# A state-space layer beside a gated MLP: the discretisation factors move from B to C, and B and C are transposed by DMA without fences

## The chip, the core and the metric

One core of a Trainium2 chip runs the whole program. The time is the device time of one execution in microseconds, the median of three runs. The core's engines work side by side: TensorE (PE) multiplies matrices, VectorE (DVE) and ScalarE (ACT) do elementwise work, GpSimd (POOL) does a little here, and SyncE (SP) issues all DMAs. Each engine carries out its own list of instructions in order and waits on semaphores for the others.

## The reference, cut to what matters

```python
xn = layernorm(x)                                  # x: 1 x 2048 x 512
dt = exp(log_dt); Lam_bar = exp(dt * Lam)          # 512 complex states
B_bar = ((Lam_bar - 1) / Lam)[:, None] * (B_re + 1j*B_im)
Bu = xn @ B_bar.T                                  # 2048 x 512, complex
h[t] = Lam_bar * h[t-1] + Bu[t]
y = 2 * real(h @ (C_re + 1j*C_im).T) + xn * Dskip
out = x + y + (gelu(xn @ w_gate) * (xn @ w_up)) @ w_down   # w: 512 x 1376, 1376 x 512
```

The factor `(Lam_bar - 1) / Lam` is one complex number for each state. It may stand on the rows of B, ahead of the recurrence, or on the columns of C, behind it: the recurrence is linear and its own factor is diagonal, so the result is the same.

## The kernel before, in words

The 2048 rows are cut into four blocks of 512. For each block b the kernel has these steps:

- **LN(b)** (lines 560 to 589): statistics (`bn_stats`, L563) and subtraction (L575) on DVE, the power on POOL (L569), the scaling `ln_mul` partly on DVE (L583) and partly on ACT (L587).
- **TR(b)** (lines 591 to 622): the transposed XNT[b]. Block 0 goes through PE; blocks 1 to 3 go through four DMA transposes each (L596).
- **GU(b)** (L676): for each of 11 tiles `ft` of the 1376 columns, four matmuls of 128x512 for the gate and four for up (L686), then on ACT the gelu (L690) and the eviction `evU` (L694), and on DVE their product `hmul` (L696). The gelu of tile ft writes one of three buffers, so it waits for the hmul of tile ft - 3.
- **BU(b)** (L624): B_bar times XNT[b], eight groups of four matmuls (L633), each evicted from PSUM by ACT (`evBu`, L637).
- **CHAIN(b)** (L640): the recurrence on DVE. The complex values are turned by tables of cosine and sine (`pre_c` L646, `pre_s` L647, `pre_re`, `pre_im`), scanned in eight real scans (L657), and turned back (`post_c` L669 to `post_im` L673).
- **DN(b)** (L704): for each of four row tiles, 11 matmuls with w_down, 4 small ones for Dskip and 8 with the transposed C (L730). DVE adds x (L742), and SP stores.

PSUM has eight banks, used in turn by all groups of matmuls: a group waits until the eviction of the eighth group before it is done.

**B.** Before, the factor is put on B while it is transposed. B_re and B_im are loaded as they are (L435). DVE makes 12 diagonal 128x128 matrices `diag` out of the factor (L514). PE multiplies slices of B by them, 64 matmuls of 128x128 called `prepB` (L533), which transposes and scales in one step, and ACT evicts the eight results (`evB`, L538). These pieces are put between the tiles of GU(0) from ft 4 on.

**C.** C_re and C_im are transposed by DMA from HBM (L450), unscaled, after everything that the first part loads.

**Tables.** `tables_fn` (L545) makes the sine and cosine tables: DVE steps, then `sint` on ACT (L551), then `f2` on DVE (L554), which overwrites what sint read, then `cost` on ACT (L556). pre_c needs both tables and the evictions of BU(0).

**Fences.** `S.dma(..., fenced=True)` makes a DMA wait for all earlier DMAs, and all later ones wait for it (lines 122 to 131). All DMA transposes are fenced.

**The order.** A planner (`schedule`, L136) holds PE's and SP's instructions in the order in which the program lists them, and chooses ACT's and DVE's order by estimated costs and due times. An edit thus changes the order on ACT and DVE beyond its own lines. Memory of the first part (raw B, diagonals, tables' steps) is reused later for the states `SS` and for CHAIN's temporaries, so the first evictions of BU(0) wait until the raw data there has been read.

PE's order is: warm-up, TR(0), GU(0) with prepB, BU(0), BU(1), GU(1), BU(2), DN(0), GU(2), DN(1), BU(3), GU(3), DN(2), DN(3).

Of the kernel before, what the change touches and what calls it, by code (L numbers as in the profile page):

```python
# [313 lines left out]
def build(nc, ins, out, dbg=None, stage=99, opts=None):  # L314
    dbg = dbg or {}
    opts = opts or {}
    with ExitStack() as es:
        E = es.enter_context
        S = Sched(nc, es)
        S.fence_slack = float(opts.get("fence_slack", FENCE_SLACK))  # L320
# [60 lines left out]
        BN = A.alloc("BN", [2, KP, D], BF16)  # L381
        DG = A.alloc("DG", [KP, 3, 128], BF16)
# [19 lines left out]
        if "DN" in dbg:  # L402
            DNB = A.alloc("DNB", [4, D], F32)
# [7 lines left out]

        do_ssm = stage >= 3
# [13 lines left out]
        if do_ssm:  # L426
            for T_, nm in ((LDT, "A_log_dt"), (LRE, "A_Lambda_re"), (LIM, "A_Lambda_im")):
                S.dma(ld_param(T_, ins[nm]), 1024, writes=[T_], tag="ld_" + nm)
# [4 lines left out]
        if do_ssm:  # L433
            for c, nm in enumerate(("A_B_re", "A_B_im")):
                S.dma(lambda e, c=c, nm=nm: e.dma_start(BN.ap[:, c], ins[nm].rearrange("(s p) d -> p s d", p=128)),  # L435
                      512 * 1024, writes=[A.sub(BN, "BN%d" % c, c)], tag="ld_" + nm)
# [8 lines left out]
        XT_DMA = opts.get("xt_dma", (1, 2, 3))  # L445

        def load_CT():
            CTc = [A.sub(CT_all, "CTc%d" % c, c) for c in range(2)]
            for c, nm in enumerate(("A_C_re", "A_C_im")):
                S.dma(lambda e, c=c, nm=nm: e.dma_start_transpose(CTc[c].ap, ins[nm]),  # L450
                      opts.get("ct_bytes", 2.0) * 512 * 1024, writes=[CTc[c]], tag="tr_" + nm, fenced=True)
# [10 lines left out]
        if do_ssm:  # L462
            POOL(lambda e: e.iota(IOTJ.ap, [[1, 512]], base=0, channel_multiplier=0), 600, [], [IOTJ], "iotj")
# [13 lines left out]
        last_table_op = None  # L477
        GATE = {"before_gelu": []}
        if do_ssm:
            (A_, TH, RRr, LBR, LBI, N1, TAa, TBb, DEN, RDEN, TC, TD, NRE, TE, TF, NIM, CR, CI) = range(18)  # L480
            pa = lambda i: PA[i].ap
            t1 = ACT(lambda e: e.activation(DTB.ap, LDT.ap, ACTF.Exp), d_act(4), [LDT], [DTB], "exp_dt")
            V(lambda e: e.tensor_tensor(pa(A_), DTB.ap, LRE.ap, ALU.mult), D_TINY, [DTB, LRE], [PA[A_]])
            V(lambda e: e.tensor_tensor(pa(TH), DTB.ap, LIM.ap, ALU.mult), D_TINY, [DTB, LIM], [PA[TH]])
            t2 = ACT(lambda e: e.activation(pa(RRr), pa(A_), ACTF.Exp), d_act(4), [PA[A_]], [PA[RRr]], "exp_a", after=[t1])
            w16 = lambda a, b_: W16.ap[:, a:b_]
            W16p = [A.sub(A.alloc("W16v", [4, 4], F32, at=W16.lo), "W16_%d" % i, i) for i in range(4)]
            V(lambda e: e.tensor_scalar(w16(0, 4), pa(TH), 1.0 / TWO_PI, None, ALU.mult), D_TINY, [PA[TH]], [W16p[0]])
            V(lambda e: e.tensor_scalar(w16(4, 8), pa(TH), 512.0 / TWO_PI, None, ALU.mult), D_TINY, [PA[TH]], [W16p[1]])
            V(lambda e: e.tensor_scalar(w16(8, 16), w16(0, 8), 0.25, None, ALU.add), D_TINY, W16p[0:2], W16p[2:4])  # L490
            V(lambda e: e.tensor_copy(KI.ap, W16.ap), D_TINY, W16p, [KI])
            V(lambda e: e.tensor_tensor(FRC.ap, W16.ap, KI.ap, ALU.subtract), D_TINY, W16p + [KI], [FRC])
            t3 = ACT(lambda e: e.activation(SC16.ap, FRC.ap, ACTF.Sin, scale=SIN_SCALE), d_act(16), [FRC], [SC16], "sin16", after=[t2])
            GATE = {"before_gelu": [t3]}
            sinT, sinP, cosT, cosP = (SC16.ap[:, 4 * i:4 * i + 4] for i in range(4))
            V(lambda e: e.tensor_tensor(pa(LBR), pa(RRr), cosT, ALU.mult), D_TINY, [PA[RRr], SC16], [PA[LBR]])
            V(lambda e: e.tensor_tensor(pa(LBI), pa(RRr), sinT, ALU.mult), D_TINY, [PA[RRr], SC16], [PA[LBI]])
            V(lambda e: e.tensor_scalar(pa(N1), pa(LBR), -1.0, None, ALU.add), D_TINY, [PA[LBR]], [PA[N1]])
            V(lambda e: e.tensor_tensor(pa(TAa), LRE.ap, LRE.ap, ALU.mult), D_TINY, [LRE], [PA[TAa]])
            V(lambda e: e.tensor_tensor(pa(TBb), LIM.ap, LIM.ap, ALU.mult), D_TINY, [LIM], [PA[TBb]])  # L500
            V(lambda e: e.tensor_tensor(pa(DEN), pa(TAa), pa(TBb), ALU.add), D_TINY, [PA[TAa], PA[TBb]], [PA[DEN]])
            V(lambda e: e.reciprocal(pa(RDEN), pa(DEN)), 150, [PA[DEN]], [PA[RDEN]])
            V(lambda e: e.tensor_tensor(pa(TC), pa(N1), LRE.ap, ALU.mult), D_TINY, [PA[N1], LRE], [PA[TC]])
            V(lambda e: e.tensor_tensor(pa(TD), pa(LBI), LIM.ap, ALU.mult), D_TINY, [PA[LBI], LIM], [PA[TD]])
            V(lambda e: e.tensor_tensor(pa(NRE), pa(TC), pa(TD), ALU.add), D_TINY, [PA[TC], PA[TD]], [PA[NRE]])
            V(lambda e: e.tensor_tensor(pa(TE), pa(LBI), LRE.ap, ALU.mult), D_TINY, [PA[LBI], LRE], [PA[TE]])
            V(lambda e: e.tensor_tensor(pa(TF), pa(N1), LIM.ap, ALU.mult), D_TINY, [PA[N1], LIM], [PA[TF]])
            V(lambda e: e.tensor_tensor(pa(NIM), pa(TE), pa(TF), ALU.subtract), D_TINY, [PA[TE], PA[TF]], [PA[NIM]])
            V(lambda e: e.tensor_tensor(pa(CR), pa(NRE), pa(RDEN), ALU.mult), D_TINY, [PA[NRE], PA[RDEN]], [PA[CR]])
            V(lambda e: e.tensor_tensor(pa(CI), pa(NIM), pa(RDEN), ALU.mult), D_TINY, [PA[NIM], PA[RDEN]], [PA[CI]])  # L510
            DGs = [[A.sub(A.sub(DG, "DGs%d" % s, s), "DG%d_%d" % (s, q), q) for q in range(3)] for s in range(KP)]
            for s in range(KP):
                for q, (src_i, fac) in enumerate(((CR, 2.0), (CI, 2.0), (CI, -2.0))):
                    V(lambda e, s=s, q=q, src_i=src_i, fac=fac: e.tensor_scalar(  # L514
                        DGs[s][q].ap, IDN.ap, PA[src_i].ap[:, s:s + 1], fac, ALU.mult, ALU.mult),
                      d_dve_ts4x(128), [IDN, PA[src_i]], [DGs[s][q]], "diag")

            BNc = [A.sub(BN, "BN%d" % c, c) for c in range(2)]

            PREP_ITEMS = []  # L520

            def prep_fn():
              for c in range(2):
                  for dk in range(KD):
                    def item(c=c, dk=dk):
                      bank = next_bank()
                      pairs = ((0, 0), (1, 2)) if c == 0 else ((1, 0), (0, 1))

# [224 lines left out]
        if do_ssm:  # L753
            PREP_holder()
# [34 lines left out]
        if do_ssm:  # L789
            BU(2); CHAIN(2)  # L790
# [79 lines left out]
```

## Time and profile before

| what | value |
|---|---|
| median of three runs | 191.8 us (191.75 to 192.15) |
| span of the profiled execution | 190.1 us |
| PE busy | 183.3 us (96%) |
| DVE busy | 152.9 us (80%) |
| ACT busy | 88.6 us (47%) |
| prepB: 64 matmuls on PE (L533) | 4.2 us busy |
| evB: 8 evictions on ACT (L538) | 4.3 us busy |
| diag: 12 on DVE (L514) | 2.0 us busy |
| DMA of C_re, C_im: issue to landing | 4.0 and 4.1 us |

The profile comes from one execution. Its times count from the start of its span, and its span is shorter than the measured time by what lies around it: 191.8 - 190.1 = 1.7 us, taking the median. The PE row counts each matmul from its start to its modelled end, so neighbouring ones overlap; in the chain of work that ended last, the same 64 prepB matmuls have four pieces of 0.89 us.

### The profile page before, as it was taken

Reading aid. Unit: us, or ns where it says so; the run is one execution under the profiler, and the core shown is the slowest. Engines: PE = TensorE matmul, PEld = TensorE weight load, DVE = VectorE, ACT = ScalarE, POOL = GpSimd, SP = SyncE. Lnnn points to the kernel's source line nnn. Section 1 sums busy time; section 2 is a strip of 40 time slices with the busy share of each in tenths; the row PEclk is TensorE's granted clock in tenths of the full one; section 3 lists DMA queues with packets and bytes.
Section 4 is the critical chain, followed back from the end, with each engine's and each line's share of the span. In section 5 each row is a group of like instructions: output and inputs, shape, how many; then the busy total and the mean of one; then the engine's idle time right before and its main releaser. Section 6 shows DMA issues by size and latency. Waiting matters only on the chain.

```text
span 190.1 us, 2549 instructions
## 1 busy us (share of the span) xinstructions
PE 183.3 (96%) x944; PEld 87.6 (46%) x944; DVE 152.9 (80%) x265; ACT 88.6 (47%) x149; POOL 5.0 (3%) x10
## 2 busy tenths in 40 slices
PE   3989999999999999999999999999999999999993
PEld 1434664444444444444444444444444444444451
DVE  5869887089999999999999989999999999411111
ACT  2297988899996473000567910017676304000000
POOL 1200200002000000000002000000000000000000
PEclk9999999999999999999999999999999999999999
DMA  4899212784422000000000221000000000100100
GB/s 111 212 349 347 49 28 55 245 276 112 110 55 55 3 0 0 28 28 31 28 2 0 54 48 41 28 33 22 0 3 0 0 0 0 55 31 32 51 28 29
DMA packets 22908, 12.26 MB, mean 64 GB/s; under 512 B 13328, under 2 KB 22896, under 8 KB 22896
## 3 DMA queue, kind: packets, MB, share of 16 engines
q1 hardware_dynamic: 22896, 12.10, 22.7%
q8 instruction: 7, 0.11, 0.2%
q14 instruction: 5, 0.04, 0.1%
HBM read 7.38 MB, written 2.10 MB: 50 GB/s over the span
## 4 chain that ended last, share of the span: by engine, by line
PE 96%; DMA 1%; DVE 1%; issue 0%; DVEq 0%
PE PS L686 40%; PE PS L730 36%; PE PS L633 15%; PE PS L769 3%; PE PS L533 2%; DMA arena<-in_A_x_dram 1%; PE PS L609 0%; DVE arena L616 0%; DVE arena L742 0%; DVEq L281 0%
## 5 line engine op out<-in xcount | busy, mean ns | idle before, releaser
L686 PE MATMUL PS<-arena 128*128 128x512 bf16 (+1 forms) x352 | 77.3, 379 | 0.9 <-DVE arena L616 0.9
L730 PE MATMUL PS<-arena 128*128 128x512 bf16 (+2 forms) x368 | 69.8, 351 | 0.0
L686 PEld LDWEIGHTS PS<-arena 128*128 128x128 bf16 (+1 forms) x352 | 35.0, 100 | 40.7 <-issue 1.0
L730 PEld LDWEIGHTS PS<-arena 128*128 128x128 bf16 (+1 forms) x368 | 33.3, 98 | 35.9
L690 ACT ACTIVATE arena<-PS 128x512 bf16<-128x512 f32 (+1 forms) x44 | 26.4, 599 | 35.1 <-PE PS L686 23.3
L657 DVE TENSOR_TENSOR_SCAN arena<-arena 128x512 bf16<-128x512 f32 x32 | 38.5, 1253 | 0.0
L694 ACT ACTIVATE arena<-PS 128x512 bf16<-128x512 f32 (+1 forms) x44 | 26.3, 597 | 6.7 <-PE PS L686 6.4
L742 DVE TENSOR_TENSOR arena<-PS,arena 128x512 bf16<-128x512 f32 x16 | 10.9, 685 | 21.4 <-PE PS L730 21.3
L633 PE MATMUL PS<-arena 128*128 128x512 bf16 x128 | 28.1, 379 | 0.0
L637 ACT ACTIVATE arena<-PS 128x512 bf16<-128x512 f32 x32 | 17.5, 618 | 22.4 <-PE PS L633 22.1
L696 DVE TENSOR_TENSOR arena<-arena 128x512 bf16<-128x512 bf16 (+1 forms) x44 | 17.6, 418 | 3.6 <-ACT arena L694 3.6
L633 PEld LDWEIGHTS PS<-arena 128*128 128x128 bf16 x128 | 12.5, 98 | 15.0
L563 DVE BATCH_NORM_STATS2 arena<-arena 128x6 f32<-128x512 bf16 x16 | 9.9, 679 | 1.2 <-DMA arena<-in_A_x_dram 1.2
L669 DVE TENSOR_TENSOR arena<-arena 128x4096 bf16<-128x4096 bf16 x4 | 9.1, 2286 | 0.0
L646 DVE TENSOR_TENSOR arena<-arena 128x4096 bf16<-128x4096 bf16 x4 | 9.1, 2285 | 0.0
L670 DVE TENSOR_TENSOR arena<-arena 128x4096 bf16<-128x4096 bf16 x4 | 9.1, 2286 | 0.0
L647 DVE TENSOR_TENSOR arena<-arena 128x4096 bf16<-128x4096 bf16 x4 | 9.1, 2284 | 0.0
L769 PE MATMUL PS<-arena 128*128 128x512 bf16 x16 | 5.8, 543 | 2.9 <-DMA arena<-in_A_x_dram 2.9
L587 ACT ACTIVATE arena<-arena 128x512 bf16<-128x512 bf16 x10 | 7.1, 721 | 1.6 <-DVE arena L570 1.6
L569 POOL TENSOR_TENSOR arena<-arena 128x4 bf16<-128x4 bf16 x4 | 4.0, 1010 | 98.6 <-DVE arena L565 98.6
L554 DVE SCALAR_TENSOR_TENSOR arena<-arena 128x2048 f32<-128x2048 f32 x1 | 2.3, 2292 | 4.5 <-ACT arena L551 4.5
L575 DVE TENSOR_SCALAR arena<-arena 128x512 bf16<-128x512 bf16 x16 | 5.0, 347 | 0.1
(70 smaller groups left out, 72.7 us busy)
## 6 DMA issues: line engine op xcount, KB each, us to landing
out_dram<-arena SPq DMA_DIRECT2D x16, 128.0 KB, 1.7
arena<-in_A_x_dram SPq DMA_DIRECT2D x3, 512.0 KB, 5.5
arena<-in_B_w_down_dram SPq DMA_DIRECT2D x1, 1280.0 KB, 7.5
arena<-in_B_w_gate_dram SPq DMA_DIRECT2D x2, 512.0 KB, 5.5
arena<-in_B_w_up_dram SPq DMA_DIRECT2D x2, 512.0 KB, 6.5
arena<-in_A_x_dram SPq DMA_DIRECT2D x4, 128.0 KB, 2.2
arena<-in_A_B_re_dram SPq DMA_DIRECT2D x1, 512.0 KB, 7.4
arena<-in_A_B_im_dram SPq DMA_DIRECT2D x1, 512.0 KB, 7.9
```

The lines of the kernel that those rows point to most:

```text
L563: V(lambda e, tt=tt: e.bn_stats(ST[tt].ap, X[tt].ap), d_dve_1x(512), [X[tt]], [ST[tt]], "bnst")
L633: ins_ = e.matmul(PS[bank][:, :], BBT[c][dk].ap[:, 128 * s:128 * (s + 1)], XNT[b].ap[:, dk, :], start=(dk == 0), stop=(dk == KD - 1))
L637: ACT(lambda e, bank=bank, k3=k3, s=s, c=c: e.activation(SSc[k3][s][c].ap, PS[bank][:, :], ACTF.Copy), d_act(512), [BANK[bank]], [SSc[k3][ ...
L646: V(lambda e: e.tensor_tensor(TA.ap, ssb.ap, cos4, ALU.mult), d_dve_tt2x(4096), [ssb, COST], [TA], "pre_c")
L657: V(lambda e, g=g, rb=rb, init=init: e.tensor_tensor_scan(g.ap, rb, g.ap, init, ALU.mult, ALU.add), d_dve_scan(512), [g, PA[RRr]] + ([CARc ...
L686: ins_ = e.matmul(PS[bank][0:m, :], W.ap[:, dk, 128 * ft:128 * ft + m], XNT[b].ap[:, dk, :], start=(dk == 0), stop=(dk == KD - 1))
L690: GATE["last_gelu"] = ACT(lambda e, bg=bg, kk=kk, m=m: e.activation(GG[kk].ap[0:m, :], PS[bg][0:m, :], ACTF.Gelu_apprx_tanh), d_act(512), ...
L694: ACT(lambda e, bu=bu, kk=kk, m=m: e.activation(UPB[kk].ap[0:m, :], PS[bu][0:m, :], ACTF.Copy), d_act(512), [BANK[bu]], [UPB[kk]], "evU")
L696: V(lambda e, kk=kk, m=m, ft=ft, k2=k2: e.tensor_tensor(HTt[k2][ft].ap[0:m, :], GG[kk].ap[0:m, :], UPB[kk].ap[0:m, :], ALU.mult), d_dve_tt ...
L730: ins_ = e.matmul(o_, l_, r_, start=(n == 0), stop=(n == len(mms) - 1))
L742: V(lambda e, bank=bank, ko=ko, tt=tt: e.tensor_tensor(OUTB[ko].ap, PS[bank][:, :], X[tt].ap, ALU.add), d_dve_1x(512), [BANK[bank], X[tt]] ...
L769: ins_ = e.matmul(PS[wb][:, :], IDN.ap, X[0].ap, start=True, stop=True)
```

## The change

- The factor is put on C, not on B. `CR` and `CI` are made twice as large as before at once, and a third value `NCI = -CI` is added. The 12 diag, the 64 prepB and the eight evB are gone.
- B_re, B_im, C_re and C_im are all transposed by DMA from HBM, in `load_BC`, listed after ft 2 of GU(0) and ahead of TR(1): on SP they come right behind the loads of w_gate and w_up. The plain loads of B are gone.
- `scale_C`, listed after GU(0), makes the scaled C: for each of four slices and for the real and imaginary part one step `c_im` on ACT (128x512, bf16 to f32, with a factor for each partition) and one step `c_re` on DVE (multiply by a factor and add, 128x512). The f32 results lie in four buffers in turn.
- No DMA is fenced any more. The transposes of one TR(b) still wait for one another, because each declares the whole of XNT[b] as written.
- Options and debug code are taken out; this moves no instruction.

In the changed program, ACT's order around the change is: evU of ft 9, four c_im, gelu of ft 10, four c_im, evU of ft 10, nine evBu, sint, five evBu, cost, two evBu, GU(1). In GU(1) the gelu of ft 9 stands after four evictions of BU(2), and that of ft 10 after two more. DVE's order is: LN(1) ahead of most of the small steps for the factor, the table steps, eight c_re, LN(2), f2, three of the four statistics of LN(3), pre_c.

```diff
-        BN = A.alloc("BN", [2, KP, D], BF16)
-        DG = A.alloc("DG", [KP, 3, 128], BF16)
+        CRAW_all = A.alloc("CRAW", [2, KP, D], BF16)
+        CTMP_all = A.alloc("CTMP", [4, D], F32)
...
-                S.dma(lambda e, c=c, nm=nm: e.dma_start(BN.ap[:, c], ins[nm].rearrange("(s p) d -> p s d", p=128)),
-                      512 * 1024, writes=[A.sub(BN, "BN%d" % c, c)], tag="ld_" + nm)
...
-        def load_CT():
...
-                S.dma(lambda e, c=c, nm=nm: e.dma_start_transpose(CTc[c].ap, ins[nm]),
-                      opts.get("ct_bytes", 2.0) * 512 * 1024, writes=[CTc[c]], tag="tr_" + nm, fenced=True)
+        def load_BC():
+            for dst, nms in ((BBT_all, ("A_B_re", "A_B_im")), (CRAW_all, ("A_C_re", "A_C_im"))):
+                for c, nm in enumerate(nms):
+                    b_ = CRAW[c] if dst is CRAW_all else A.sub(BBT_all, "BBTc%d" % c, c)
+                    S.dma(lambda e, b_=b_, nm=nm: e.dma_start_transpose(b_.ap, ins[nm]),
+                          2 * 512 * 1024, writes=[b_], tag="tr_" + nm)
...
+        def scale_C():
+            for s in range(KP):
+                for c, (f_im, f_re) in enumerate(((NCI, CR), (CR, CI))):
+                    t = CTMP[(2 * s + c) % 4]
+                    ACT(lambda e, s=s, t=t, f_im=f_im: e.activation(
+                        t.ap, CRAW[1].ap[:, s, :], ACTF.Copy, scale=PA[f_im].ap[:, s:s + 1]),
+                        d_act(512, 1), [CRAW[1], PA[f_im]], [t], "c_im")
+                    V(lambda e, s=s, c=c, t=t, f_re=f_re: e.scalar_tensor_tensor(
+                        CT[c][s].ap, CRAW[0].ap[:, s, :], PA[f_re].ap[:, s:s + 1], t.ap, ALU.mult, ALU.add),
+                      d_dve_1x(512), [CRAW[0], PA[f_re], t], [CT[c][s]], "c_re")
...
-                        opts.get("xt_bytes", 1.2) * 128 * 1024, reads=[XN[tt % 8]], writes=[xd], tag="tr_x%d" % b, fenced=True)
+                        1.2 * 128 * 1024, reads=[XN[tt % 8]], writes=[xd], tag="tr_x%d" % b)
...
         for ft in range(KF):
             GU(0, [ft])
-            if ft >= opts.get("prep_from", 4):
-                prep_some(2)
-            if ft == opts.get("tr1_at", 2):
+            if ft == 2:
+                load_BC()
                 TR(1)
                 late_loads()
-        prep_some(99)
-        if do_ssm:
-            load_CT()
+        scale_C()
```

## Prediction

> **What bounds the kernel now.** I read the page, then TensorE's (PE's) waits, the chain that ended last, and the timeline of VectorE (DVE) and ScalarE (ACT) from 33 to 73 us. All times are us from the start of the profiled span.
>
> ```profile
> span 190.1 us, 2549 instructions
> PE 183.3 (96%) x944; PEld 87.6 (46%) x944; DVE 152.9 (80%) x265; ACT 88.6 (47%) x149; POOL 5.0 (3%) x10
> ```
>
> PE's waits have two rows, both before 10.5 us:
>
> ```profile
> PE PS L769 <- DMA arena<-in_A_x_dram: 2.9, 1, 2.9
> PE PS L686 <- DVE arena L616: 0.9, 1, 0.9
> ```
>
> So PE sets the end and never stands still after 10.47. The chain (start, length) gives its timetable:
>
> ```profile
> 10.47 8.79 PE PS L686 x40
> 19.27 0.89 PE PS L533 x16
> ...
> 33.20 13.81 PE PS L633 x64
> 47.02 18.99 PE PS L686 x88
> 66.01 6.91 PE PS L633 x32
> 72.92 17.31 PE PS L730 x92
> ```
>
> BU(0) and BU(1) start at 33.20, GU(1) at 47.02, BU(2) at 66.01, DN(0) at 72.92. What matters is how near the others are. From the timeline:
>
> ```profile
> 35.58 1.28 ACT L551 ACT_TABLE_LOAD   x1
> 36.87 1.91 ACT L551 ACTIVATE arena<-arena 128x2048 bf16<-128x2048 f32 x1
> ...
> 38.82 2.29 DVE L554 SCALAR_TENSOR_TENSOR arena<-arena 128x2048 f32<-128x2048 f32 x1 [4.47 <-ACT arena L551]
> ...
> 46.04 2.28 DVE L646 TENSOR_TENSOR arena<-arena 128x4096 bf16<-128x4096 bf16 x1
> ...
> 70.32 1.22 DVE L673 TENSOR_TENSOR arena<-arena 128x2048 bf16<-128x2048 bf16 x1
> ```
>
> sint (ACT) releases f2 (DVE), then CHAIN(0) begins with pre_c at 46.04 and ends with post_im at 71.54, 25.5 us without a gap. DN(0) reads its result and starts at 72.92: **the slack is 1.4 us**, although the page shows no wait there. Later slacks are wide: CHAIN(1) ends at 99.8 for DN(1) at 109.2, CHAIN(2) at 134.4 for DN(2) at 152.4, CHAIN(3) at 160.7 for DN(3) at 169.8, and XNT3 lands at about 115 for BU(3) at 126.5.
>
> **Part 1, PE.** The 64 prepB matmuls go: four pieces of 0.89 in the chain, 3.56 us, all on the path. A group of four matmuls takes 18.99/22 = 0.863. If nothing else were late, PE would reach BU(0) at 29.64, BU(1) at 36.55, GU(1) at 43.46, BU(2) at 62.45, DN(0) at 69.36, and the time would be 191.8 - 3.6 = 188.2. That is the lower limit.
>
> **Part 2, DMA.** The two plain B loads (1 MB) go. Four 512x512 transposes come, issued right behind the last weight load instead of at 43.7 behind fences. The C transposes of before show their price, 4.0 and 4.1 to landing, 1.9 of issue on SP, and how long the DMA engines work:
>
> ```profile
> arena<-in_A_C_re_dram SPq DMA_TRANSPOSE x1, 4.0
> arena<-in_A_C_im_dram SPq DMA_TRANSPOSE x1, 4.1
> ```
> ```profile
> 45.00:46.00 1.00, 1.00 (x7) 0.41 (x6) 0.83 (x4) 1.00 (x3) 0.26 (x1) 1.00 1.07 241
> 46.00:47.00 1.00, 1.00 (x6) 0.47 (x5) 1.00 (x2) 0.93 (x2) 0.00 (x0) 1.00 1.22 273
> ```
>
> The last columns are DMA share and GB/s: 2.0 to 2.1 us of full engines each. The last weight load landed at 12.21 + 8.4 = 20.6; without 1 MB at the 350 GB/s of that stretch, at 17.6. How transposes queue behind loads the trace doesn't show. Lower bound: SP issues the four from 11.9 at 1.9 each, and the last lands 4.1 after its issue, at 21.7. Upper bound: each takes its whole 4.1 after the other, and the last lands at 34.0. I take the engine time, the nearest row to a full queue: 17.6 + 4 x 2.1 = 26.0. B (needed 29.64) lands at about 22, C_im at 26.0.
>
> TR(1)'s four transposes stand behind them on SP. They still wait for one another, since each declares all of XNT1 written, at 2.5 each: the last lands at 26.6 + 3 x 2.5 = 34.1, needed at 36.55. x2 and x3 follow; x3 is issued at about 34.6 and lands 8.5 later, as before, at 43.1. The fences themselves cost PE nothing (SP's wait at 20.9 ended without a PE wait), so their loss gains nothing.
>
> **Part 3, ACT.** The eight evB (pairs of 1.08) go, eight c_im come. c_im isn't in the trace: 0.48 (start to start of evictions) to 0.72 (ln_mul alone); I take the 0.60 between two ln_mul (1.32 - 0.72), the same form; at 0.72 everything below comes 1.0 later (193.0), at 0.48 up to 0.8 earlier. The evB lay spread through GU(0); the c_im stand in one block around GU(0)'s last gelu, and sint, which stood behind two BU evictions, now stands behind nine. The queue: evU of ft 9 starts at 10.47 + 20 x 0.863 + 0.10 = 27.84; c_im 1 at 28.32; four c_im, one gelu (0.48), four c_im, one evU put the first evBu at 34.08. It overwrites the memory of the raw C, so it waits for the last c_re: c_im 8 at 33.00, + 0.72 + 0.62 = 34.4, so 34.45. The ninth evBu starts at 34.45 + 8 x 0.48 = 38.29 and ends at 38.9; table load 1.28, sint 1.91: **42.1, against 38.8 before**. PE doesn't feel this (evictions lag under eight banks).
>
> **Part 4, DVE.** Twelve diag (2.04) go, eight c_re come, each between 0.35 (L575, 512 wide) and 0.69 (L742); I take a quarter of L554, 2.29/4 = 0.57, and some start-up: 0.60. They fill DVE before sint and cost nothing there: c_re end at 34.4, LN(2) starts at about 35.6 and is ready for f2 at 39.8, before sint. If c_re cost 0.69 that cover still holds. But three of LN(3)'s statistics now stand between f2 and pre_c. f2 at 42.15; f2 2.21, reciprocal to sub 0.74 (45.30 to 46.04), three BN at 0.60: pre_c at **46.9, against 46.04**. cost, two evictions, the gelu table and the first gelu and evU end at 49.7 on ACT, while DVE is through pre_c at 49.1 and waits 0.6 for that evU in hmul. Then post_im ends at 46.9 + 0.6 + 25.5 = 73.0.
>
> **Sum.** DN(0) starts at 73.05 to 73.1, against 72.92: +0.15. PE stands still for about 3.7 us before it: about 1.2 before BU(2)'s fifth group (ft 9's gelu now comes after four evictions of BU(2)), 2.2 before the seventh (ft 10's gelu waits for the hmul behind post_s) and the rest before DN(0). Behind that the wide slacks hold. Span 190.1 + 0.15 = 190.25; the runs' median 191.8 lies 1.7 above the span, so **192.0**. The whole gain of part 1 turns into a wait for CHAIN(0).
>
> One row bears on these gaps: PE was idle for 0.86 (9.61 to 10.47), and the 40 matmuls after it took 8.79, 0.22 each, with the granted clock at 1.00. [...]
>
> **Rivals.**
> - *Nearer to PE's pace.* If c_im costs 0.48, ACT catches PE up, the ninth evBu starts at 37.5, everything to pre_c comes 0.8 earlier: DN(0) at 72.3, 191.2. Without the hmul wait too, 190.6. What decides is when the ninth evBu starts. For: ACT's evictions do run at 0.48. Against: ln_mul has this form and doesn't. The full 188.2 would need a chain that starts 3.7 earlier, for which no row speaks.
> - *Transposes drain late (slower).* c_im stands in order on ACT, ahead of PE's evictions; TR(1) and x3 stand in order behind C on SP. It decides once C_im lands after 28.3, that is above 2.7 us per transpose. At 3.3 each: C_im 30.8, c_im 2.5 late; TR(1) 38.9, BU(1) 2.4 late beside it; x3 at 47.8, 0.2 more: +2.7 on +0.15, 194.7. At 4.1 each: 5.7 late, 197.7. For: 4.0 alone. Against: engines busy for only 2.1 of it.
> - *PE slows after the gaps.* After the 2.9 us of idle at the start the first 16 matmuls took 5.80, against 16 x 0.216 = 3.45 at the later pace: a slow stretch costs 2.35. Against: the gap of 0.86 was followed by none, and my gaps of up to 2.2 lie between the two. One such stretch gives 194.4.
> - *The fences were the gain.* They would show as PE waits; there are none.
>
> **How the numbers follow.** Chances: forecast 0.54 (own range 191.2 to 192.8), nearer to PE's pace 0.20 (190.6 to 191.2), late transposes 0.23, slow PE after the gaps 0.03; the last rival is inside the forecast. The measurement can tell about 0.2%, 0.4 us. Of the forecast's 0.54, 0.10 lies faster by more than that (below 191.4), 0.27 within, 0.17 slower. So faster 0.10 + 0.20 = 0.30, same 0.27, slower 0.17 + 0.23 + 0.03 = 0.43. The range runs from 190.3, below the faster rival, to 195.0, above late transposes at 3.3 each; it leaves out the drain at 4.1 and the full gain.
>
> **What would show it.** Right: no L533 rows; BU(0) at about 29.6; C landed before 28; sint ending near 42, pre_c near 46.9; PE waits of some 3.7 us at BU(2) and DN(0), released by ACT and DVE, where there were none. Wrong: a PE wait at BU(0) or BU(1) (transposes late), ACT waiting for a DMA before c_im, pre_c waiting for x3, or DN(0) clearly before 72.3, which would say that CHAIN(0) started earlier than this sum allows.

## The result, and the profile after

| kernel | median us | executions | ratio to before |
|---|---|---|---|
| before, beside it | 191.98 | 191.75 to 192.23 (4) | |
| after | 193.81 | 193.29 to 195.08 (4) | 1.011 [1.007, 1.015] |

The change makes the kernel slower by 1.8 us. The forecast was 192.0; the time lies inside the range, on its slower side. The profiled execution is the longest of the four (195.08). From its page, first what is busy, then the granted clock in 40 slices:

```profile
span 193.0 us, 2401 instructions
...
PE 181.9 (94%) x880; PEld 84.2 (44%) x880; DVE 156.2 (81%) x262; ACT 88.9 (46%) x149; POOL 5.2 (3%) x10
...
PEclk9999999999999996999999999999999999999999
```

PE has 64 instructions fewer and 1.4 us less busy time, the slow stretch described below included, and yet the span is 2.9 us longer. PE's waits now have a row that was not there:

```profile
PE PS L597 <- ACT arena L654: 4.2, 2, 2.8
PE PS L699 <- DMA arena<-in_A_x_dram: 3.0, 1, 3.0
PE PS L650 <- DVE arena L580: 0.9, 1, 0.9
```

BU(2) (L597) stands still for 4.2 us in two gaps, for the gelu (L654) that frees a PSUM bank. PE's timeline has them in brackets:

```profile
67.47 1.90 PE L597 MATMUL PS<-arena 128*128 128x512 bf16 x8 [1.33 <-ACT arena L654]
72.20 3.51 PE L597 MATMUL PS<-arena 128*128 128x512 bf16 x8 [2.83 <-ACT arena L654]
```

The chain that ended last (start, length) says what the gelu waited for:

```profile
50.89 0.43 DVE arena L659
51.32 2.20 DVE arena L611
...
66.72 2.20 DVE arena L633
68.92 2.20 DVE arena L634
71.13 0.34 DVE arena L659
...
71.56 0.60 ACT arena L654
...
72.20 3.51 PE PS L597 x8
75.71 17.39 PE PS L683 x92
93.11 18.99 PE PS L650 x88
```

Before, the chain ran on PE alone from 10.47 us to the last matmul. Now 20.7 us of it run through CHAIN(0) on DVE: from the first hmul (L659) and pre_s (L611) over post_c and post_s (L633, L634) to the hmul of GU(1)'s eighth tile, which frees the gelu's buffer. DN(0) starts at 75.71, 2.79 later than before. From there on everything takes its old time: the 92 matmuls 17.39 against 17.31, GU(2) 18.99 as GU(1) had. So the whole loss is made before DN(0).

How ACT and DVE got there, from the timeline (start, busy, engine, line; in brackets the idle time before and who ended it):

```profile
29.45 2.74 DVE L509 SCALAR_TENSOR_TENSOR arena<-arena 128x512 bf16<-128x512 bf16 x4 [1.18 <-ACT arena L506]
...
32.61 2.73 DVE L509 SCALAR_TENSOR_TENSOR arena<-arena 128x512 bf16<-128x512 bf16 x4
...
35.42 4.51 ACT L601 ACTIVATE arena<-PS 128x512 bf16<-128x512 f32 x9 [0.85 <-issue]
...
37.45 2.47 DVE L532 BATCH_NORM_STATS2 arena<-arena 128x6 f32<-128x512 bf16 x4 [1.14 <-DMA arena<-in_A_x_dram]
...
41.25 1.91 ACT L520 ACTIVATE arena<-arena 128x2048 bf16<-128x2048 f32 x1
...
43.19 2.29 DVE L523 SCALAR_TENSOR_TENSOR arena<-arena 128x2048 f32<-128x2048 f32 x1 [1.52 <-ACT arena L520]
...
47.93 2.28 DVE L610 TENSOR_TENSOR arena<-arena 128x4096 bf16<-128x4096 bf16 x1
...
50.89 0.43 DVE L659 TENSOR_TENSOR arena<-arena 128x512 bf16<-128x512 bf16 x1 [0.68 <-ACT arena L657]
...
72.93 1.22 DVE L637 TENSOR_TENSOR arena<-arena 128x2048 bf16<-128x2048 bf16 x1
```

The last c_re (L509) ends at 35.34; the first evBu (L601) follows at 35.42, after 0.85 us in which ACT stood still. The view names no releaser for this wait; that it was the last c_re is tested by run 6. sint (L520) ends at 43.16, f2 (L523) waits 1.52 for it, pre_c (L610) starts at 47.93 (before: 46.04), and the first hmul (L659) holds pre_s back by another 0.68. post_im (L637) ends at 74.15 (before: 71.54). DVE works through CHAIN(0) without another gap.

The second loss is in PE's windows of 1 us (columns: the stretch, its length, PE's busy time, granted clock, DMA share, GB/s):

```profile
71.00:72.00 1.00, 0.00 (x0) 1.00 0.00 0
72.00:73.00 1.00, 0.80 (x3) 0.66 0.00 0
73.00:74.00 1.00, 1.00 (x4) 0.50 0.00 0
74.00:75.00 1.00, 1.00 (x4) 0.50 0.00 0
75.00:76.00 1.00, 1.00 (x4) 0.63 0.00 0
76.00:77.00 1.00, 1.00 (x7) 1.00 0.00 0
```

After the gap of 2.83 us the clock is at 0.50 for 3.41 us, and the eight matmuls there take 3.51 us, against 1.90 for the eight before them: 1.6 us. Two of the four executions show a mean clock of 0.991 (195.08 and 194.34), two of 0.998 (both 193.29); the first two took 1.0 and 1.8 us longer. (The profiled executions of runs 3 and 7 show 0.998 as well, and there the last two groups of BU(2) take 1.90 us each: the clock had not fallen.)

### The profile page after: what moved, and what is told of

The parts are those of the page before. It is cut to its first block, busy times and chain, and to the rows that moved or that the text cites. A ratio compares the mean times of both kernels' runs of the same rounds, so it can differ in the third digit from the quotient of the medians.

```text
span 193.0 us, 2401 instructions
## 1 busy us (share of the span) xinstructions
PE 181.9 (94%) x880; PEld 84.2 (44%) x880; DVE 156.2 (81%) x262; ACT 88.9 (46%) x149; POOL 5.2 (3%) x10
## 4 chain that ended last, share of the span: by engine, by line
PE 61%; DVE 11%; ACT 0%; issue 0%; DVEq 0%
PE PS L683 36%; PE PS L650 20%; PE PS L597 5%; DVE arena L621 5%; DVE arena L659 1%; DVE arena L634 1%; DVE arena L633 1%; DVE arena L611 1%; DVE arena L614 1%; DVE arena L612 1%; DVE arena L688 0%; ACT arena L654 0%; DVE arena L627 0%; DVEq L281 0%
## 5 line engine op out<-in xcount | busy, mean ns | idle before, releaser
L654 ACT ACTIVATE arena<-PS 128x512 bf16<-128x512 f32 (+1 forms) x44 | 26.6, 605 | 34.9 <-PE PS L650 22.6
L597 PE MATMUL PS<-arena 128*128 128x512 bf16 x128 | 30.1, 395 | 4.2 <-ACT arena L654 4.2
L601 ACT ACTIVATE arena<-PS 128x512 bf16<-128x512 f32 x32 | 17.7, 607 | 27.2 <-PE PS L597 26.3
L597 PEld LDWEIGHTS PS<-arena 128*128 128x128 bf16 x128 | 12.7, 100 | 20.6 <-ACT arena L654 5.1
L659 DVE TENSOR_TENSOR arena<-arena 128x512 bf16<-128x512 bf16 (+1 forms) x44 | 17.7, 416 | 2.3 <-ACT arena L657 2.2
L633 DVE TENSOR_TENSOR arena<-arena 128x4096 bf16<-128x4096 bf16 x4 | 9.1, 2284 | 0.0
L610 DVE TENSOR_TENSOR arena<-arena 128x4096 bf16<-128x4096 bf16 x4 | 9.1, 2283 | 0.0
L611 DVE TENSOR_TENSOR arena<-arena 128x4096 bf16<-128x4096 bf16 x4 | 9.1, 2283 | 0.0
L634 DVE TENSOR_TENSOR arena<-arena 128x4096 bf16<-128x4096 bf16 x4 | 9.1, 2282 | 0.0
L699 PE MATMUL PS<-arena 128*128 128x512 bf16 x16 | 5.8, 544 | 3.0 <-DMA arena<-in_A_x_dram 3.0
L509 DVE SCALAR_TENSOR_TENSOR arena<-arena 128x512 bf16<-128x512 bf16 x8 | 5.5, 746 | 1.2 <-ACT arena L506 1.2
```

The lines of the kernel that those rows point to most:

```text
L597: ins_ = e.matmul(PS[bank][:, :], BBT[c][dk].ap[:, 128 * s:128 * (s + 1)], XNT[b].ap[:, dk, :], start=(dk == 0), stop=(dk == KD - 1))
L601: ACT(lambda e, bank=bank, k3=k3, s=s, c=c: e.activation(SSc[k3][s][c].ap, PS[bank][:, :], ACTF.Copy), d_act(512), [BANK[bank]], [SSc[k3][ ...
L611: V(lambda e: e.tensor_tensor(TB.ap, ssb.ap, sin4, ALU.mult), d_dve_tt2x(4096), [ssb, SINT], [TB], "pre_s")
L633: V(lambda e: e.tensor_tensor(TA.ap, ssb.ap, cos4, ALU.mult), d_dve_tt2x(4096), [ssb, COST], [TA], "post_c")
L634: V(lambda e: e.tensor_tensor(TB.ap, ssb.ap, sin4, ALU.mult), d_dve_tt2x(4096), [ssb, SINT], [TB], "post_s")
L654: GATE["last_gelu"] = ACT(lambda e, bg=bg, kk=kk, m=m: e.activation(GG[kk].ap[0:m, :], PS[bg][0:m, :], ACTF.Gelu_apprx_tanh), d_act(512), ...
```

## The experiments

The times of before beside these runs were 191.9 to 192.1. Ratios are to before. In what follows "DN(0) starts" is from PE's timeline, where before has 72.75.

**1. The fences alone.** Before, without any fence:

```diff
-  ... tag="tr_" + nm, fenced=True)
+  ... tag="tr_" + nm)
-  ... tag="tr_x%d" % b, fenced=True)
+  ... tag="tr_x%d" % b)
```

> The kernel before with its fences taken away and nothing else (the planner then moves a few instructions on VectorE and ScalarE). Chain theory (the end is set by CHAIN(0), which hangs on the place of sint): sint stays behind two evictions of BU(0), PE has no wait before DN(0), so the time stays within 0.4 us of before (191.6 to 192.4). Rival, the fences matter: their loss alone moves the time, by 1 us or more to one side.

Measured: 192.38 (192.08 to 192.67), ratio 1.0016 [1.0007, 1.0025]. DN(0) starts at 73.02, and PE's waits are the two old ones and one of 0.7 in TR(0). The fences cost nothing that PE felt; without them the time is 0.3 longer, and that part lies outside the span (see the last section).

**2. The change with the fences kept.**

```diff
-                          2 * 512 * 1024, writes=[b_], tag="tr_" + nm)
+                          2 * 512 * 1024, writes=[b_], tag="tr_" + nm, fenced=True)
-                        ... tag="tr_x%d" % b)
+                        ... tag="tr_x%d" % b, fenced=True)
```

> The changed kernel with the fences put back on all transposes. Worked out: the four transposes run one after another behind the last weight load (17.6 + 4 x 4.1 = 34 us), TR(1) behind them until 44, so BU(1) waits for XNT1 some 7.5 us where it started at 36.7; part of that is what CHAIN(0) would have made PE wait anyway. Chain theory: DN(0) at about 77, 196 us. Rival, transposes side by side with loads were what made the changed kernel late: with fences it gets faster than 193.3.

Measured: 203.02 (202.50 to 203.46), ratio 1.057 [1.055, 1.059], worse than worked out. The largest wait of PE, and SP's issue of TR(1):

```profile
PE PS L597 <- ACT arena L601: 10.3, 1, 10.3
```
```profile
36.01 9.28 SPq L560 DMA_TRANSPOSE arena<-arena  x4
```

PE stands still ahead of BU(1), until 46.76. The view names ACT's evictions, but the one that BU(1)'s first group needs ended at 43.35. TR(1), fenced behind C_im, was issued from 36.01 to 45.29 (in after from 24.60 to 33.63), and its last transpose lands behind that: PE waited for XN(1). ACT was late as well, since the planner put cost and all eight c_im ahead of BU(0)'s evictions (from 42.75; in after from 35.42).

In the long wait the granted clock was halved as well, from 40.88 to 51.12 us, so that the matmuls from 46.76 on ran at half pace for 4.4 us.

So the loss of the fences is a condition of the change, not a gain of its own: with them, and with the order that the planner then chooses, the changed kernel is 11 us slower than before.

**3. Is it sint's place?** After, with sint behind the second eviction of BU(0), as before had it, in place of the ninth:

```diff
+        put("scalar", find("scalar", "sint"), find("scalar", "evBu", 1))
```

> The changed kernel with one instruction moved on ScalarE: sint stands behind the second eviction of BU(0), as before, not behind the ninth. Chain theory: sint ends near 39.7, f2 then starts when LN(2) lets it, near 41.7 and not 43.2, and all of CHAIN(0) comes 1.5 us earlier; DN(0) near 72.7, PE's long wait before BU(2)'s seventh group falls from 2.8 to about 1.3 us, and with it the clock's fall, so all executions lie near 191.8. Rival, late transposes and loads set the chain: no change, 193.3 to 195.1. Rival, the scaling of C by its own cost: no change either.

Measured: 193.45 (193.33 to 194.07), ratio 1.0077 [1.0062, 1.0092]: a miss. sint came at 37.65, but the cosine table did not come earlier with it:

```profile
45.19 2.03 ACT L525 ACTIVATE arena<-arena 128x2048 bf16<-128x2048 f32 x1
...
47.31 2.29 DVE L610 TENSOR_TENSOR arena<-arena 128x4096 bf16<-128x4096 bf16 x1 [0.66 <-ACT arena L525]
...
50.62 0.42 DVE L659 TENSOR_TENSOR arena<-arena 128x512 bf16<-128x512 bf16 x1 [1.01 <-ACT arena L657]
```

cost (L525) still stands behind twelve more evictions, pre_c gains 0.6, the first hmul 0.3. PE waited 1.9 us in BU(1) for the evictions behind sint, and DN(0) started at 73.94. From this I took the theory that ACT's queue from 28 to 50 us is full, and the c_im in it too much.

**4. Does the gap halve the clock?** After, with twelve matmuls without use put into PE's long gap:

```diff
+                    if b == 2 and (s, c) == (3, 0):
+                            for _ in range(12):
+                                ins_ = e.matmul(PS[fb][:, :], IDN.ap, XNT[2].ap[:, 0, :], start=True, stop=True)
```

> The changed kernel with 12 extra matmuls of 128x512 on PE ahead of BU(2)'s seventh group, into the bank of DN(0)'s first tile, which overwrites them (12 x 0.216 = 2.6 us, inside the wait of 2.83). If the idle time is what halves the clock in some executions: all executions near 193.3, granted clock 1.00 behind the gap. If it is not: executions up to 195 with a clock of 0.99 remain. If the wait is not idle time but hidden work: about 2.6 us slower, 195.9.

Measured: 193.48 (193.40 to 194.04), ratio 1.0083 [1.0068, 1.0099], a clock of 0.998 or 1.000 in all six executions.

```profile
69.04 2.75 PE L601 MATMUL PS<-arena 128*128 128x512 bf16 x11
72.04 1.90 PE L608 MATMUL PS<-arena 128*128 128x512 bf16 x8 [0.24 <-ACT arena L665]
74.04 6.23 PE L694 MATMUL PS<-arena 128*128 128x512 bf16 x31
```

With the gap filled (L601) the last two groups of BU(2) (L608) take 1.90 in place of 3.51. So without the gap there is no slow clock, in six of six executions, and without it the change still loses 1.5 us.

**5. Hardly any work in the scaling on ACT.** After, every instruction in its place, but C is scaled for one column of 512; the other columns of the scaled C are zero, so that part of the computation is left out.

```diff
-                        t.ap, CRAW[1].ap[:, s, :], ACTF.Copy, scale=PA[f_im].ap[:, s:s + 1]),
+                        t.ap[:, 0:1], CRAW[1].ap[:, s, 0:1], ACTF.Copy, scale=PA[f_im].ap[:, s:s + 1]),
...
+                        e.memset(CT[c][s].ap[:, 1:], 0.0)
+                        return e.scalar_tensor_tensor(
+                            CT[c][s].ap[:, 0:1], CRAW[0].ap[:, s, 0:1], PA[f_re].ap[:, s:s + 1], t.ap[:, 0:1], ALU.mult, ALU.add)
```

> The changed kernel with every instruction in its place, but the scaling of C is done for one column of 512 (the other 511 columns of the scaled C are set to zero, so that part of the computation is left out): c_im falls from 0.60 us to some 0.2 and c_re's place takes some 0.3 us in place of 0.67. Theory (ACT's queue from 28.5 to 50 us is full, and the scaling, 4.8 us of c_im and the wait for the last c_re, pushes the rotation tables and GU(1)'s first evictions back): evBu's first starts near 32 (35.42), the first gate product of GU(1) near 47.5 (50.89), PE's gap of 2.8 us before BU(2)'s 7th group is gone, DN(0) starts between 69.4 and 71.5 (75.71), about 190 us (188.3 to 191.5). Rival, DVE's additions behind 37 us (LN(3)'s statistics) or the late x2 and x3 set the end: hmul and DN(0) hardly move, 193 us.

Measured: 194.50 (193.59 to 194.90), ratio 1.0115 [1.0077, 1.0152]. The theory of a full ACT queue falls: c_im took 0.29 us, and nothing was won. Three of the four executions show the clock's fall; the fourth, 193.59, is no better than after's 193.29. On DVE the zeros cost nearly as much as the scaling did: a memset of 0.48 us and a step of 0.10, 0.55 from one pair to the next, against 0.67 for c_re.

```profile
38.55 2.47 DVE L534 BATCH_NORM_STATS2 arena<-arena 128x6 f32<-128x512 bf16 x4 [3.77 <-DMA arena<-in_A_x_dram]
...
42.68 2.28 DVE L525 SCALAR_TENSOR_TENSOR arena<-arena 128x2048 f32<-128x2048 f32 x1
```

Now DVE stands still for 3.77 us for x2, which came 1.1 us later here than in after. LN(2) comes at 38.55, f2 stands behind LN(2) on DVE (42.68, without waiting for sint), and it is now cost on ACT that waits 0.99 for DVE. pre_c is at 47.40. Two queues are late at the same time; what is taken from ACT's shows DVE's.

**6 to 8. One of the two queues at a time.** Their expectations were written before number 5 was measured and still hold its theory of a full ACT queue. Number 6 gives raw C memory of its own and keeps every order, so that only the wait of the first evBu for the last c_re is gone:

```diff
+        FAR = A.alloc("CRAWFAR", [2, KP, D], BF16)
...
+            CRAW[c].ap = FAR.ap[:, c]
...
+                o.deps = [d for d in o.deps if d.tag not in own]     # own: c_im, c_re and C's transposes; o: evBu
```

> The changed kernel with raw C and its buffers in memory of their own, so that the first eviction of BU(0) need not wait for the last c_re; the order on every engine is the same. Theory (a full ACT queue): the eviction starts near 34.3 in place of 35.42 and everything on ACT to 50 us comes about 1.0 earlier, DN(0) near 74.7; c_im's 4.8 us still stand in the queue, so only that much: 192.3 us (191.8 to 193.0). Were the wait for c_re the whole cause: 191 or less. If DVE is the cause: 193.3.

Measured: 193.07 (192.44 to 194.48), ratio 1.0065 [1.0038, 1.0092]. This lies just above the range worked out.

```profile
34.23 4.43 ACT L601 ACTIVATE arena<-PS 128x512 bf16<-128x512 f32 x9
...
46.66 2.27 DVE L610 TENSOR_TENSOR arena<-arena 128x4096 bf16<-128x4096 bf16 x1
```

The first evBu starts at 34.23, 1.2 earlier; f2 at 41.92 and pre_c at 46.66 come as much earlier. So the first evBu had waited for the last c_re, and the wait was handed down to pre_c. In the time it is worth less: 0.7 us by the medians, and 0.3 if only executions without the clock's fall are compared (192.99 against 193.29).

Number 7 moves LN(3)'s three statistics from ahead of pre_c to behind CHAIN(0):

```diff
+        put("vector", [find("vector", "bnst", n) for n in (12, 13, 14)], find("vector", "post_im", 0))
```

> The changed kernel with LN(3)'s first three statistics moved on DVE from between f2 and pre_c to behind CHAIN(0). Theory (ACT's queue): pre_c can start only after the cosine table at 47.5, and hmul's first still waits for ACT until 50.9, so no gain: 193.3 us (193.0 to 193.8). Rival (DVE's own additions, 1.8 us of statistics, are what delays the chain): 191.5 us.

Measured: 195.41 (194.00 to 195.66), ratio 1.015 [1.011, 1.020]: no gain, as the expectation said of DVE's own additions, and a loss that it did not foresee. Much of the loss is the clock: three of the four executions (195.39 to 195.66) show a mean clock of 0.989 or 0.990. The profiled one, without the fall, took 194.00, 0.7 more than after's 193.29, and PE waited 0.7 there for a DMA transpose ahead of BU(1).

```profile
39.40 2.47 DVE L532 BATCH_NORM_STATS2 arena<-arena 128x6 f32<-128x512 bf16 x4 [3.38 <-DMA arena<-in_A_x_dram]
...
47.92 2.29 DVE L610 TENSOR_TENSOR arena<-arena 128x4096 bf16<-128x4096 bf16 x1 [1.37 <-ACT arena L525]
```

DVE was free for pre_c 1.37 us earlier and waited for cost (L525). x2 landed at 39.4 in this execution, against 37.4 in that of after; why its landing moves by 2 us these runs don't tell.

Number 8 puts c_im on DVE, in bf16, with raw C apart, in the planner's order but for two c_re and the Dskip diagonals:

```diff
-                    ACT(lambda e, s=s, t=t, f_im=f_im: e.activation(
-                        t.ap, CRAW[1].ap[:, s, :], ACTF.Copy, scale=PA[f_im].ap[:, s:s + 1]),
+                    V(lambda e, s=s, t=t, f_im=f_im: e.tensor_scalar(
+                        t.ap, CRAW[1].ap[:, s, :], PA[f_im].ap[:, s:s + 1], None, ALU.mult),
```

> The changed kernel with c_im on DVE (bf16 in and out, about 0.25 us each) in place of ACT, raw C in memory of its own, and the planner's own order except that the last two c_re and the Dskip diagonals stand right behind the other c_re on DVE. Theory (ACT's queue): ACT is free from 30.5, evicts BU(0) from 31 to 33 on, the sine table stands ahead of it, pre_c starts near 42.5 in place of 47.9, hmul's first near 46.5, PE runs without a gap into DN(0) at about 69.4 (before: 72.92), which gives back the 3.56 us of the B preparation: 188.4 us (187.8 to 189.8), faster than both. Rival (DVE's load sets the end): the scaling adds 2 us to DVE before 37 us, and CHAIN(0) ends no earlier than 74, 193 us or more.

Measured: 192.23 (191.88 to 193.21), ratio 1.0021 [0.9998, 1.0043]: 1.6 better than after, not 5; 1.2 better if only executions without the clock's fall are compared (192.11). ACT is early (cost ends at 39.5), but now DVE is full: four c_im take 1.14 us there (the 0.25 each of the expectation was an estimate), c_re and c_im run until 41.2, and LN(2), which no longer waits for x2, starts at 41.77. pre_c at 46.78.

**9. The scaling on POOL.** The third theory, that DN(0) waits for CHAIN(0), and that CHAIN(0) starts when the later of two queues is through, asks for an engine that is in neither. Two products and a sum for each of the eight blocks, and the orders changed by hand as the expectation says:

```diff
+                    POOL(lambda e, s=s, t=t, f_im=f_im: e.tensor_scalar(
+                        t.ap, CRAW[1].ap[:, s, :], PA[f_im].ap[:, s:s + 1], None, ALU.mult),
...
+                    POOL(lambda e, s=s, u=u, f_re=f_re: e.tensor_scalar(
+                        u.ap, CRAW[0].ap[:, s, :], PA[f_re].ap[:, s:s + 1], None, ALU.mult),
...
+                    POOL(lambda e, s=s, c=c, t=t, u=u: e.tensor_tensor(CT[c][s].ap, t.ap, u.ap, ALU.add),
```

> The scaling of C goes to POOL (two scalings and one addition for each of the eight blocks), raw C has memory of its own, and by hand on DVE: no LN(3) statistics ahead of pre_c, hmul of GU(1)'s first tile behind pre_s, those of its 7th and 8th ahead of post_c, and on ACT the 11th tile's gelu ahead of BU(2)'s evictions. The theory of a full ACT queue fell with the one-column run; the new theory: DN(0) waits for CHAIN(0) on DVE, which is in order and takes 25.5 us from pre_c to post_im without waits (before: 46.04 to 71.54), and pre_c comes after two queues that are late at the same time, x2's landing (37.4 to 39.4) with LN(2), f2 and LN(3)'s statistics behind it on DVE, and c_im, the evictions, sint and cost on ACT; taking one away shows the other. Here both go: pre_c at 42.5 to 44.5, post_im's end at 68 to 70, DN(0) at 69.4 to 70, 188.6 us (188.0 to 190.0) if POOL takes some 1.2 us an instruction and DVE is not slowed by it; 190 to 192 if DVE's operations grow while POOL works. Rival, a bound that is neither (PE's own, the loads): 192 or more.

Measured: 203.44, ratio 1.057 [1.052, 1.062]: a miss by far, since POOL is slow and slows DVE. Groups by line (busy, mean ns of one), PE's waits, and two rows of DVE's timeline:

```profile
L512 POOL TENSOR_SCALAR arena<-arena 128x512 f32<-128x512 bf16 x8 | 21.9, 2744 | 13.0 <-DVE arena L499 13.0
...
L515 POOL TENSOR_TENSOR arena<-arena 128x512 bf16<-128x512 f32 x8 | 13.3, 1684 | 0.0
```
```profile
PE PS L688 <- POOL arena L515: 5.6, 1, 5.6
```
```profile
57.26 0.84 DVE L664 TENSOR_TENSOR arena<-arena 128x512 bf16<-128x512 bf16 x1
...
77.50 2.28 DVE L642 TENSOR_TENSOR arena<-arena 128x2048 bf16<-128x2048 bf16 x1
```

The last sum ends at 80.9 and DN(0) waits 5.6 us for it. DVE's hmul (L664) takes 0.84 in place of 0.40 and post_im (L642) 2.28 in place of 1.22 while POOL works. It goes both ways: beside DVE's two products of 128x4096, POOL's L512 took 5.0 and 5.2 us, against 1.6 to 1.9 in most other places. One hmul of 0.84 us ran from 57.26 to 58.10, inside a POOL operation that ran from 57.12 to 58.70, so there DVE went on at half its pace (spans on POOL are rough); the hmul that began at 51.77 took 1.49. Why each slows the other these rows don't show. No run shows the 1.2 us that the expectation set for a POOL instruction: the three kinds took 2.74, 1.87 and 1.68 in the mean.

**10. Orders alone, the scaling at its full cost.** Raw C apart, c_im and c_re kept in after's places, sint behind the second eviction, f2 ahead of LN(2), no LN(3) statistics ahead of pre_c, the hmuls of GU(1) moved away from where DVE waits for them:

```diff
+        put("scalar", [find("scalar", "sint")], find("scalar", "evBu", 1))
+        put("scalar", [find("scalar", "cost")], find("scalar", "evBu", 8))
...
+        put("vector", [find("vector", "hmul", 10)] + [find("vector", "dgsk", n) for n in range(4)] + [find("vector", "f2")], c_re[7])
+        put("vector", [find("vector", "hmul", 11)], find("vector", "pre_s", 0))
+        put("vector", [find("vector", "hmul", 17)], find("vector", "scan", 5))
+        put("vector", [find("vector", "hmul", 18)], find("vector", "scan", 7))
```

> The scaling stays on ACT and DVE, in the changed kernel's place and at its full cost; raw C has memory of its own, and only orders are changed: sint behind the second eviction of BU(0) and f2 ahead of LN(2), so that both of the late queues end sooner; no LN(3) statistics ahead of pre_c; hmul of GU(1)'s first tile behind pre_s, its 7th and 8th ahead of post_c, the 11th tile's gelu ahead of BU(2)'s evictions. New theory (CHAIN(0) on DVE, started late by two queues together): f2 near 37.5, LN(2) to 44.6, pre_c near 44.6, post_im's end near 70.2, PE waits up to 1.9 us in BU(1) for evictions behind sint, DN(0) at 70.2 to 71.3, 190.3 us (189.5 to 191.3). Rival (the scaling's work itself is what costs): 193 or more.

Measured: 191.91 (191.65 to 192.39), ratio 0.999 [0.998, 1.001]; 1.9 us below after (1.4 below its executions without the clock's fall), 1.6 above what was worked out.

```profile
38.66 2.29 DVE L524 SCALAR_TENSOR_TENSOR arena<-arena 128x2048 f32<-128x2048 f32 x1 [2.60 <-ACT arena L521]
...
46.02 2.28 DVE L611 TENSOR_TENSOR arena<-arena 128x4096 bf16<-128x4096 bf16 x1
```
```profile
PE PS L684 <- DVE arena L638: 1.9, 1, 1.9
```

The loss of the change is gone with all of its work still there, so the rival "the work itself costs" falls. PE's one long wait behind GU(0) is now at DN(0) (L684): 1.9 us for post_im (L638). Two short ones, 0.5 and 0.3, lie in BU (L598). pre_c starts at 46.02, as before the change, because DVE stood still for 2.60 us for a sint that comes behind eight c_im.

**11 and 12. The work split between ACT and DVE.** Four c_im on ACT, four on DVE, sint directly behind GU(0); one hmul behind each step of CHAIN(0). Number 12 also issues x2 ahead of TR(1).

```diff
+                    if s >= 2:
+                        V(lambda e, s=s, t=t, f_im=f_im: e.tensor_scalar(
...
+        put("scalar", [find("scalar", "sint")], find("scalar", "evU", 10))
+        put("scalar", [find("scalar", "cost")], find("scalar", "evBu", 5))
...
+        for n, (tag, k) in enumerate((("pre_s", 0), ("pre_re", 0), ("pre_im", 0), ("scan", 0), ("scan", 1), ("scan", 2), ("scan", 3), ("scan", 4))):
+            put("vector", [hm[11 + n]], find("vector", tag, k))
```
```diff
                 load_BC()
+                ld_x(2)
                 TR(1)
```

> The work of the change in full, spread so that neither ACT nor DVE is late: raw C in memory of its own; four c_im on ACT ahead of GU(0)'s last gelu, the other four on DVE in bf16; sint directly behind GU(0)'s last eviction, f2 ahead of LN(2), cost behind the 6th eviction of BU(0); no LN(3) statistics ahead of pre_c; one hmul of GU(1) behind each of pre_s, pre_re, pre_im and the first five scans. If CHAIN(0) on DVE is what DN(0) waits for: c_re ends near 36, f2 near 38.2, LN(2) starts with x2 (37.4 to 39.4) and takes 5.0, pre_c at 43.2 to 44.5 (46.02 in the run with orders alone), post_im's end 26 later at 69.2 to 70.5, PE without a gap over 1 us, DN(0) at 69.6 to 70.6: 189.2 us (188.5 to 190.2). If the bound is elsewhere: no better than the run with orders alone, 191.9.

> The same with the load of x2 issued ahead of the transposes of XN(1) in place of behind them. LN(2) then starts when f2 ends (38.2) and not when x2 lands; against that stands up to 2 us of traffic ahead of the transposes of XN(1), which had about 2 us to spare. 188.9 us (188.3 to 190.0), 0 to 0.7 below the run without this move.

Measured: number 11 190.16 (189.51 to 190.32), ratio 0.990 [0.989, 0.992], faster than before and after, at the slow edge of what was worked out. Number 12 190.47 (189.88 to 190.70), ratio 0.991 [0.990, 0.993]: not told apart from 11, a miss. PE's last wait in each:

```profile
PE PS L692 <- DVE arena L646: 0.8, 1, 0.8
```
```profile
PE PS L605 <- DMA arena<-arena: 2.1, 1, 2.1
```

In 11, pre_c starts at 44.69 and DN(0) waits 0.8 for post_im:

```profile
44.69 2.28 DVE L619 TENSOR_TENSOR arena<-arena 128x4096 bf16<-128x4096 bf16 x1
```

LN(2) started there at 39.68 directly behind f2, without a wait for x2, so the move in 12 had nothing to win. It put off TR(1), whose issue on SP ended at 37.0 in place of 34.6, and PE waits 2.1 us for it ahead of BU(1). DN(0) comes at 71.29 against 70.79.

The runs that bear on CHAIN(0) side by side, from the timelines; the last column takes only executions without the clock's fall ahead of DN(0), that is with a mean clock of 0.997 or more:

| kernel | pre_c starts | wait of first hmul | post_im ends | DN(0) starts | median us | median without the fall |
|---|---|---|---|---|---|---|
| before | 46.04 | 0 | 71.54 | 72.75 | 191.98 | 191.98 |
| after | 47.93 | 0.68 | 74.15 | 75.50 | 193.81 | 193.29 (2 of 4) |
| 5, one column scaled | 47.40 | 0.69 | 73.62 | 74.86 | 194.50 | 193.59 (1 of 4) |
| 6, raw C apart | 46.66 | 0.69 | 72.88 | 73.87 | 193.07 | 192.99 (5 of 8) |
| 8, c_im on DVE | 46.78 | 0.33 | 72.66 | 72.72 | 192.23 | 192.11 (7 of 10) |
| 10, orders | 46.02 | 0 | 72.21 | 72.27 | 191.91 | 191.91 (10 of 10) |
| 11, split | 44.69 | 0.37 | 70.74 | 70.79 | 190.16 | 190.16 (5 of 5) |

post_im's end minus pre_c's start minus the wait is 25.5 in the first five rows and 25.7 in number 11. In number 10 it is 26.2; its second hmul waited 0.42. In all but before, which still had PE's own pace, DN(0) starts directly behind post_im or behind a stretch of slow clock.

## Why the prediction was right in its mechanism and 1.8 us short

- **PE (part 1): right.** BU(0) was worked out for 29.64 and started at 29.60, GU(1) 43.46 and 43.41, BU(2) 62.45 and 62.52. The times worked out are from the chain, the measured ones from PE's timeline, where before has 33.04, 46.85 and 65.84; so 3.4, 3.4 and 3.3 of the 3.56 us are saved as far as BU(2).
- **DMA (part 2): nearly right.** C_im was to land at 26.0 and landed at 27.0, under the 28.3 from which it would matter. The rival of late transposes did not come: no wait at BU(0) or BU(1). x3 landed at 43.1, as worked out. Not foreseen: LN(2) waited 1.14 us for x2 and started at 37.45 instead of 35.6. In after this was hidden behind sint; run 5 showed what it costs once that cover is gone.
- **ACT and DVE (parts 3 and 4): the failed step.** I took 0.60 for c_re and wrote "If c_re cost 0.69 that cover still holds". Of the cover on DVE that was true; but the first evBu overwrites raw C and waits for the last c_re, and that was worked out with the c_im as the slower of the two. c_re came 0.67 apart, behind one another with hmul and a diagonal between the two fours, and ended at 35.34, not 34.4. Of these 0.9 us some 0.4 came with the c_im, the eighth of which ended at 34.10 and not at 33.72; the rest is the queue of c_re on DVE. The first evBu came 0.97 late, sint ended at 43.16 (42.1), f2 started at 43.19 (42.15), pre_c at 47.93 (46.9): the same second is handed down. Run 6 took this wait away and moved pre_c by 1.27. The rest stood: the hmul's wait 0.68 (0.6), the chain 25.5, post_im's end 74.15 (73.0).
- **The gaps.** 1.33 and 2.83 us at the two groups of BU(2) that were named (1.2 and 2.2 worked out), released by the gelu as described.
- **The clock: a rival weighed too lightly.** "PE slows after the gaps" had 0.03, since the longest gap was worked out at 2.2 us and the one of 0.86 had been followed by no slow stretch. It came in two of four executions, which took 1.0 and 1.8 us longer; in PE's row it cost 1.6. The rival's price, 2.35, was read from PE's first matmuls, where before's profile shows a granted clock of 1.00 (2 to 9 us), so that row was no such fall. Run 4 confirmed that it takes the gap. A gap of the length worked out would not have been safe either: in run 6 the clock fell behind one of 2.08.
- **Outside the span.** I kept 1.7 us around the span; the executions of after have 2.08. Together: 1.15 from CHAIN(0) and 0.38 outside give 193.5 for 192.0, where the executions without the slow clock show 193.29; the clock in half of them makes the median 193.81.

The range and the sign that was likeliest (slower, 0.43) held; "within" and "faster" had too much, since three errors of the same sign were left out. That the range held is partly luck: the forecast's own range ended at 192.8, and the room from there to 195.0 had been left for late transposes, which did not come.

## What to carry to other kernels

When an engine that sets the pace is freed of some work, look for the next chain that is already nearly as late: here CHAIN(0) had 1.4 us of slack, so 3.56 us off PE could bring 1.4 at most while CHAIN(0) stayed where it was, and the new work was put in the queues that start that chain. Two queues that meet in one instruction hide one another: taking the cost out of one (runs 3, 5, 7) brought nothing until both were reordered (runs 10 and 11). New memory for a buffer and a look at what each engine's list waits for in order was worth 3.6 us by the medians, 3.1 without the clock's fall (after to run 11), with no work left out.

## What the runs showed of the hardware that was not expected

- A gap of 2.83 us, and in run 6 one of 2.08 us, was enough to halve PE's clock, in some executions of the same kernel and not in others: 2 of 4 in after, 3 of 4 in runs 5 and 7, 3 of 8 in run 6, 3 of 10 in run 8 show a mean clock of 0.989 to 0.991. The length of the gap does not decide alone: the profiled execution of run 7 has the same gap of 2.83 us and that of run 8 one of 2.79, and behind both the group took 1.90. The traces show how long a fall lasts: the granted clock stood at 0.50 for 3.41 us in after (from 72.33), run 5 (from 71.23) and run 6 (from 71.44), for 10.24 = 3 x 3.41 us in run 2 and for 17.07 = 5 x 3.41 us in run 9. And the fall doesn't come with the end of the gap: in after it came 0.13 us behind it, in run 6 0.50 us behind it, when PE was at work again, in run 5 0.45 us ahead of it. How much idle time it takes, and what makes the executions differ, no run here settles.
- The issue of a DMA transpose behind other transfers held SP for longer: in after, that of B_re, right behind the loads of the weights, kept SP for 6.06 us, the next ones 2.1 to 3.2, against 1.8 to 1.9 for C's in before, which stood alone. What holds SP there the traces don't show. So late landings were less to be feared than SP's own time: everything listed behind, TR(1) and x2, moves with it.

```profile
10.84 6.06 SPq L441 DMA_TRANSPOSE arena<-in_A_B_re_dram  x1
16.95 2.31 SPq L441 DMA_TRANSPOSE arena<-in_A_B_im_dram  x1
19.30 3.15 SPq L441 DMA_TRANSPOSE arena<-in_A_C_re_dram  x1
```

- The time around the span is 1.80 us in before and 1.83 in run 2, the two kernels with fences, and 2.07 to 2.11 in all twelve without (means of each kernel's executions). That is the whole of run 1's 0.3 us. What happens there the profile doesn't show, and it stays open.
- Beside a busy DVE, POOL's 128x512 operations took 1.7 to 2.7 us each in the mean (run 9); of DVE's own, post_im took 2.28 in place of 1.22, and hmul 0.84 to 1.49 in several places, in place of 0.40.
